# Linformer attention and a gated feed-forward net on one core: gates and every output block by seven products, attention outputs multiplied from PSUM, and an order of instructions and banks that a list scheduler gives

## The chip, the cores and the metric

The kernel runs on one core of a Trainium2 chip. The metric is device time in microseconds (us) of one execution. Five engines share the work: TensorE (PE) multiplies, ScalarE (ACT) and VectorE (DVE) work elementwise on SBUF and PSUM, GpSimd (POOL) broadcasts rows and issues the loads on its queue, SyncE (SP) issues transposes, small gathers and the stores.

## What is computed

Eight batch entries, eight heads, 1024 positions, head size 64; keys and values are first projected to 64 rows, and the attention's result goes through a gated net:

```python
k_proj = einsum('ks,bhsd->bhkd', E, k)
v_proj = einsum('ks,bhsd->bhkd', F, v)
attn = softmax(matmul(q, k_proj^T) / sqrt(64))
x = matmul(attn, v_proj)             # -> (8192 tokens, 512)
gate = sigmoid(x @ w_gate)           # w_gate, w_val: (512, 1536)
out = (gate * (x @ w_val)) @ w_out   # w_out: (1536, 512) -> (8192, 512) float32
```

Matmuls take bfloat16 and add up in float32. The sigmoid is had from tanh(x/2), so hidden values are (tanh + 1) times the value product, and the factor 0.5 is put on at the output.

## The kernel before

**Tiling.** The 8192 tokens are 16 blocks of 512, two for each batch entry. A block needs, for each of 12 chunks of 128 hidden columns, a gate product and a value product (each 4 matmuls of 128x512), and then the output product over 1536. Twelve chunks are handled as three quads of four: a quad holds chunks 2q, 2q+1, 2q+6 and 2q+7, so that it is a 2x2 problem in halves of the columns, halves of the depth and halves of the tokens.

**Seven products.** The value half of a quad is done by Winograd's form of Strassen's scheme: seven products of half-size operands, each four matmuls of 128x256, in place of eight (`v_pieces`, L1502, with `v_product`, L1421). The operands are sums of weights (`vt_sums`, L1372, once) and of tokens (`xs_sums`, L1411, for each block). Sums of products are in part had by further accumulation in the same PSUM bank: a bank collects P1, then P2's relatives on top; ACT takes a copy of it in between (`v_snap`, L1470) and DVE adds another bank to that copy (`v_add`, L1473, recorded at L1476). DVE then multiplies by the gates (`hidden`, L1449, recorded at L1457). The output of blocks 1 to 15 goes the same way (`first_products` L1282, `last_products` L1301, `add_snap` L1264, recorded at L1267); the last block has an order of its own with one more bank (`final_products`, L1318). The **gates** are direct: `g_step` (L1484) does one chunk with four 128x512 matmuls and one tanh. **Block 0** is direct throughout, its output too (`oproj`, L1146: 12 matmuls of 128x512 for each 128 tokens).

**Attention of one entry** (`attention`, L801) is made while the net works on the entry before. Keys and values are projected in one bank (`kv`, L754; 64x64 tiles of the array); kpd is transposed by a DMA of SP into kpD; q is transposed by four DMAs of SP into qT (`transpose_q`, L741). Scores are 64x64 matmuls, four abreast in the array, exponentials by ACT; denominators by 32-wide tiles, reciprocals by DVE, gathered into rows by SP's DMAs and spread over the partitions by POOL (`spread`, L921, recorded at L926). The outputs of attention are kept by ACT in SBUF as xu (`x_half`, L991) and multiplied there by DVE with the spread reciprocals into xT (`mul`, L954, recorded at L958). Heads go in four pairs r = 0..3; three pairs' scores stand in one event, the fourth pair's scores with the first two outputs in the next, the outputs of the last two pairs in a third (`scores3`, `mixed3`, `outputs3`). Entry 1 is made in the first stage, with its keys transposed and its reciprocals spread by PE (`k_alone`, `bc`).

**What sets the order.** A `Plan` (L28) records operations with what they read and write and makes the semaphores; each engine runs its own in the order of recording. That order is written out by hand: the first entry's slots in `todo`, later entries six quads with hooks (`on`, L1656 and on), so a g_step stands between each two steps of a value quad. PSUM's eight banks are two rings, FF for the net and AA for attention and output, with free lists. `mm` (L264) records every matmul, `act` (L268) every ACT operation, `load` (L282) every load on POOL's queue, so in the profile nearly all matmuls have the line L264, and groups are told apart by tiles. (pF and pA are the banks, wG and wV the weights, vT their sums, xT the tokens, xS their sums, hT the hidden values, hS their sums, wT the sums of w_out.)

**Loads.** At the start POOL queues entry 0's keys, queries and values in halves, then the weights in pieces. `second_loads` (L1584) queues q, k, v of entry 1, asks SP for q's transposes, and then w_out, which waits for two of those transposes; then the library of the broadcast. Later entries' k waits for the four transposes of the entry before, since both lie in one area with the spread reciprocals.

Of the kernel before, what the change touches and what calls it, by code (L numbers as in the profile page):

```python
# [27 lines left out]
class Plan:  # L28
# [9 lines left out]
    def add(self, eng, fn, r=(), w=(), x=(), dma=None):  # L38
# [5 lines left out]
        def dep(o, raw):  # L44
            if o is op:
                return
            if o.eng == eng and o.dma is None:
                if eng == "PE" or (eng != "POOL" and not raw):
                    return
            deps[id(o)] = o  # L50
# [67 lines left out]

def bass_linformer_attn__then__ffn_glu_sigmoid_kernel(
# [15 lines left out]
    NR = H // 2  # L135
    SCALE = 1.0 / (DH ** 0.5)

    with contextlib.ExitStack() as es:
# [4 lines left out]

        vT = sbuf("vT", [P, 3, 2, DFF // 2], BF16)
        wT = sbuf("wT", [P, 4, NF // 2, 256], BF16)
        early = [vT[:, :, :, :].rearrange("p a b c -> p (a b c)")]
        used = [0]

        def within(shape, dtype):
# [41 lines left out]
        )  # L191
        kpd = sbuf("kpd", [64, H, 2, DH], BF16)
        kpD = sbuf("kpD", [P, H, DH], BF16)
        vpD = sbuf("vpD", [P, H, DH], BF16)
# [3 lines left out]
        rrow = (  # L198
            eT[:, :, :].rearrange("p n c -> p (n c)").bitcast(FP32)
            .rearrange("p (i c) -> p i c", i=4)  # L200
        )
        xu = sbuf("xu", [P, 8, 512], FP32)
        xT = [sbuf(f"xT{i}", [P, NI, 2, 512], BF16) for i in range(2)]

        wG = sbuf("wG", [P, NI, DFF], BF16)
        wV = sbuf("wV", [P, NI, DFF], BF16)
        wO = sbuf("wO", [P, NF, DM], BF16)
        sigs = [sbuf(f"sig{i}", [P, 2, 512], FP32) for i in range(3)]
        sig = [sigs[i][:, 0, :] for i in range(3)]
        hT = [sbuf(f"hT{i}", [P, NF, 512], BF16) for i in range(2)]  # L210
        ost = sbuf("ost", [P, 4, DM], FP32)
        hS = sbuf("hS", [P, 2, NF // 2, 256], BF16)
        snap = [EF[:, 0:512], EF[:, 512:1024], sbuf("snap2", [P, 512], FP32)[:, :]]
        vsnap = [sbuf(f"vsnap{i}", [P, 512], FP32) for i in range(3)]
        xS = [sbuf(f"xS{i}", [P, 4, 2, 256], BF16) for i in range(2)]

# [4 lines left out]
        FB, AB = (0, 1, 2, 3), (4, 5, 6, 7)  # L221

        plan = Plan()
        add = plan.add
# [10 lines left out]
        A0, A1, A2, A3 = AB  # L235
        F0, F1, F2, F3 = FB
# [8 lines left out]
        ffn, att = Ring(FB), Ring(AB)  # L245

        class Free(list):
            def take(self):
                return self.pop(0)

            def two(self):
                return [self.pop(0), self.pop(0)]

        FF, AA = Free(), Free()

        def mm(b, o, lhsT, rhs, r, start=True, stop=True, tp=None, tr=False, read=False):
# [7 lines left out]
            return add("PE", lambda e: e.matmul(o, lhsT, rhs, **kw), r=r, x=[("bank", b)])  # L264

        def act(o, i, r, w, b=None, func=AF.Copy, scale=1.0):
            x = [] if b is None else [("bank", b)]
            return add("ACT", lambda e: e.activation(o, i, func, scale=scale), r=r, w=w, x=x)  # L268

        def dve(fn, r, w, b=None):  # L270
            x = [] if b is None else [("bank", b)]
            return add("DVE", fn, r=r, w=w, x=x)

        def pool(fn, r=(), w=()):
            return add("POOL", fn, r=r, w=w)


        wg_v = moe_w_gate.rearrange("(i p) f -> p i f", p=P)
        wv_v = moe_w_val.rearrange("(i p) f -> p i f", p=P)

        def load(o, i, w, sem, r=()):
            add("POOL", lambda e: e.dma_start(o, i), r=r, w=w, dma=sem)  # L282
# [4 lines left out]
        def load_k(b, after=()):  # L287
            n = 0
            load(
                KV[n][:, :, :],  # L290
                k[b].rearrange("h (p t) d -> p h (t d)", t=NT),
                [("KV", n, 0), ("KV", n, 1)],
                f"KV{n}",
                r=(turned() if b >= 2 else []) + list(after),
            )

        def load_v(b):
            n = 1
            load(
                KV[n][:, :, :],  # L300
                v[b].rearrange("h (p t) d -> p h (t d)", t=NT),
                [("KV", n, 0), ("KV", n, 1)],
                f"KV{n}",
            )
# [10 lines left out]
        def load_q(b):  # L315
            load(
                Qb[:, :, :],
                q[b].rearrange("h (p t) d -> p h (t d)", t=NT),
                [("Q", hf, R) for hf in range(2) for R in range(2)],
                "Q",  # L320
            )
# [10 lines left out]
        WCH = (0, 256, 512, 768, 1024, 1280, 1536)  # L332

        def load_w(j, ih=None):
            c = slice(WCH[j], WCH[j + 1])
            ii = slice(0, NI) if ih is None else slice(2 * ih, 2 * ih + 2)
            for n, t, src in (("wG", wG, wg_v), ("wV", wV, wv_v)):
                load(
                    t[:, ii, c],
                    src[:, ii, c],  # L340
                    [(n, j, x) for x in ((0, 1) if ih is None else (ih,))],
                    f"{n}{j}" if ih is None else f"{n}{j}h{ih}",
                )


        def start_loads():
            for src, rows, n in ((E, slice(0, 64), "E"), (F, slice(64, 128), "F")):
                add(
                    "SP",
                    lambda e, src=src, rows=rows: e.dma_start(EF[rows, :], src[:, :]),  # L350
# [139 lines left out]

        def busy(n):
            for _ in range(n):
                mm(FB[3], bank[FB[3]][:, 0:P], ident[:, :], ident[:, :], ["ident"])

        def pairs(R):
            return slice(0, NR) if R is None else slice(2 * R, 2 * R + 2)

        def both(R):  # L500
# [1327 lines left out]
```

## Time and profile before

| what | value |
|---|---|
| time, median of 3 runs (lowest to highest) | 532.36 us (531.95 to 533.25) |
| span of the profiled execution, slowest core | 529.3 us |
| its own time outside the span | not given; the median is 3.1 us over the span |
| PE busy, start to last end | 5.5 to 526.2 us in the span |
| ACT and DVE, busy share | 58% and 79% |
| matmuls of gates: pF<-xT,wG 128x512 | 707 recorded, 186.8 us busy |
| DVE addition to a copy, L1476, 128x512 | 689 ns each |
| ACT copy of a bank to vsnap, 128x512 | 598 ns each |
| ACT tanh of a bank, 128x512 | 601 ns each |
| DVE multiplication xT<-xu,KVs, L958 | 1023 ns each |
| POOL broadcast, L926 | 1035 ns each |
| bytes over the DMA queues | 56.18 MB, mean 106 GB/s |

How to read it: the span runs from the first to the last instruction that the profiler recorded. "Busy" counts the time in which an engine has an instruction under way; as PE's matmuls are pipelined and their ends modelled, its busy time says little of its pace, and the pace is read from one start to the next. A group in the profile is all instructions of one line, engine, operation and tile; behind it stand the busy time, the mean of one, and what ended the idle time before. The share of the chain that ended last says which engine the end hangs on. A DMA's "us to landing" runs from its issue to its last byte. The clock column is the share of full speed that was granted to PE; it reads 1.00 in every stretch named here.

### The profile page before, as it was taken

The page shows a single profiled execution, that of the slowest core. Times are in us where ns is not written, and L with a number is a line of the kernel's source. Part 1 is how long each engine was busy: PE and PEld are TensorE (multiplying, and loading weights), DVE is VectorE, ACT ScalarE, POOL GpSimd, SP SyncE. Part 2 cuts the span into 40 slices and gives each one's busy share as a digit, 9 for nine tenths or more (in the row PEclk, how much of TensorE's full clock was granted, in tenths as well). Part 3 has the DMA queues.
Part 4 walks back from the last instruction along what each step waited for, and adds up shares of the span by engine and source line. Part 5 has one row for each costly group of instructions (what it writes and reads, how often), then busy time and mean ns, then how long its engine had stood idle before and what let it go on. Part 6 is the DMA issues. An engine that isn't in the chain of part 4 may idle for free.

```text
span 529.3 us, 10415 instructions
## 1 busy us (share of the span) xinstructions
PE 515.5 (97%) x4110; PEld 350.8 (66%) x4173; DVE 416.3 (79%) x681; ACT 307.2 (58%) x551; POOL 133.4 (25%) x148
## 2 busy tenths in 40 slices
PE   5999999999999999999999999999999999999997
PEld 4545646656857667585766767576685867677676
DVE  4549786788987788877988779877888788997855
ACT  2565753688385564946468474764838564554541
POOL 9310200106700085001920048100650009200000
PEclk9999999999999999999999999999999999999999
DMA  9999999994393255911589223962620020202022
GB/s 167 199 199 202 155 213 195 184 171 89 35 230 60 82 91 84 231 53 38 90 157 162 80 40 57 213 105 80 88 86 1 0 83 3 80 1 79 1 81 80
DMA packets 77154, 56.18 MB, mean 106 GB/s; under 512 B 34801, under 2 KB 69297, under 8 KB 77105
## 3 DMA queue, kind: packets, MB, share of 16 engines
q0 software_dynamic: 33984, 29.89, 36.6%
q1 hardware_dynamic: 43120, 25.63, 19.4%
q8 instruction: 32, 0.52, 0.4%
q14 instruction: 18, 0.14, 0.1%
HBM read 60.29 MB, written 16.78 MB: 146 GB/s over the span
## 4 chain that ended last, share of the span: by engine, by line
PE 90%; DMA 7%; issue 1%; POOL 1%; DVE 0%; ACT 0%; POOLq 0%
PE pF L264 59%; PE pA L264 31%; DMA wO<-in_moe_w_out_dram 2%; DMA qT<-Qb 2%; DMA KVs<-in_v_dram 2%; POOL KVs L282 0%; POOL Qb L282 0%; DVE rden L639 0%; DVE vsnap L1476 0%; ACT vsnap L268 0%; DVE ost L1338 0%; POOL quad L356 0%; POOLq L102 0%; POOLq L1813 0%
## 5 line engine op out<-in xcount | busy, mean ns | idle before, releaser
L264 PE MATMUL pF<-xT,wG 128*128 128x512 bf16 x707 | 186.8, 379 | 3.8 <-DMA wG<-in_moe_w_gate_dram 0.2
L926 POOL PARTITION_BROADCAST KVs<-eT x96 | 96.8, 1035 | 243.5 <-PE pF L264 190.7
L268 ACT ACTIVATE sig<-pF 128x512 f32<-128x512 f32 x192 | 115.4, 601 | 49.3 <-PE pF L264 47.3
L1476 DVE TENSOR_TENSOR vsnap<-pF,vsnap 128x512 f32<-128x512 f32 x135 | 93.0, 689 | 39.7 <-PE pF L264 29.5
L264 PEld LDWEIGHTS pF<-xT,wG 128*128 128x128 bf16 x768 | 74.2, 98 | 54.5 <-issue 1.7
L268 ACT ACTIVATE vsnap<-pF 128x512 f32<-128x512 f32 x135 | 80.7, 598 | 46.9 <-PE pF L264 42.4
L1457 DVE SCALAR_TENSOR_TENSOR hT<-sig,vsnap 128x512 bf16<-128x512 f32 x135 | 93.5, 693 | 6.2
L264 PE MATMUL pF<-xT,wV 128*128 128x256 bf16 (+1 forms) x408 | 66.9, 286 | 0.0
L264 PE MATMUL pA<-wO,hT 128*128 128x256 bf16 x534 | 63.4, 273 | 0.0
L264 PEld LDWEIGHTS pA<-wO,hT 128*128 128x128 bf16 x534 | 52.1, 98 | 6.6 <-DVE ost L1267 0.3
L264 PE MATMUL pF<-xS,wV 128*128 128x256 bf16 x360 | 54.1, 273 | 0.3
L264 PEld LDWEIGHTS pF<-xT,wV 128*128 128x128 bf16 x408 | 38.2, 98 | 23.9 <-issue 5.7
L264 PE MATMUL pF<-xS,vT 128*128 128x256 bf16 x360 | 54.0, 273 | 0.0
L264 PEld LDWEIGHTS pF<-xS,wV 128*128 128x128 bf16 x360 | 34.3, 98 | 25.6 <-DVE vsnap L1476 5.0
L958 DVE TENSOR_TENSOR xT<-xu,KVs 128x512 bf16<-128x512 f32 x48 | 47.4, 1023 | 1.2 <-POOL KVs L926 0.7
L268 ACT ACTIVATE EF<-pA 128x512 f32<-128x512 f32 x30 | 17.9, 597 | 46.9 <-PE pA L264 46.9
L264 PE MATMUL pA<-wT,hT 128*128 128x256 bf16 x360 | 44.2, 273 | 0.0
L264 PE MATMUL pA<-wT,hS 128*128 128x256 bf16 x360 | 41.7, 273 | 0.0
L264 PEld LDWEIGHTS pA<-wT,hT 128*128 128x128 bf16 x360 | 35.1, 98 | 7.4 <-ACT snap L268 0.3
L264 PEld LDWEIGHTS pA<-wT,hS 128*128 128x128 bf16 x360 | 35.1, 98 | 4.3 <-issue 0.2
L264 PEld LDWEIGHTS pF<-xS,vT 128*128 128x128 bf16 x360 | 35.2, 98 | 4.1
L1267 DVE SCALAR_TENSOR_TENSOR ost<-pA,EF 128x512 f32<-128x512 f32 x29 | 20.0, 688 | 19.8 <-PE pA L264 19.7
(113 smaller groups left out, 487.6 us busy)
## 6 DMA issues: line engine op xcount, KB each, us to landing
out_dram<-ost SPq DMA_DIRECT2D x60, 256.0 KB, 2.4
Qb<-in_q_dram POOLq DMA_DIRECT2D x7, 1024.0 KB, 20.5
KVs<-in_k_dram POOLq DMA_DIRECT2D x7, 1024.0 KB, 12.0
KVs<-in_v_dram POOLq DMA_DIRECT2D x7, 1024.0 KB, 16.2
wO<-in_moe_w_out_dram POOLq DMA_DIRECT2D x1, 1536.0 KB, 12.3
wG<-in_moe_w_gate_dram POOLq DMA_DIRECT2D x5, 256.0 KB, 17.9
wV<-in_moe_w_val_dram POOLq DMA_DIRECT2D x5, 256.0 KB, 18.5
KVs<-in_k_dram POOLq DMA_DIRECT2D x2, 512.0 KB, 7.8
```

The source lines that it names most:

```text
L264: return add("PE", lambda e: e.matmul(o, lhsT, rhs, **kw), r=r, x=[("bank", b)])
L268: return add("ACT", lambda e: e.activation(o, i, func, scale=scale), r=r, w=w, x=x)
L926: lambda e, n=n, i=2 * rnd + c, j=j, parts=parts: e.partition_broadcast(rb[0:parts, n, :], rrow[32 * j : 32 * j + 1, i, :], channels=parts),
L958: lambda e: e.tensor_tensor(xT[s][:, r, :, 256 * g : 256 * g + 256], xu[:, n, :].rearrange("p (f c) -> p f c", f=2), y.rearrange("p (f c) ...
L1267: lambda e: e.scalar_tensor_tensor(o, bank[bk][:, :].rearrange("p (j c) -> p j c", j=2), 0.5, snap[n].rearrange("p (j c) -> p j c", j=2), ...
L1457: lambda e: e.scalar_tensor_tensor(o, sg[:, :, cc], 1.0, x.rearrange("p (j c) -> p j c", j=2), ALU.add, ALU.mult,),
L1476: lambda e: e.tensor_tensor(o, bank[bk][:, :], o, ALU.add),
```

## The change

The kernel computes the same; `kernel(...)` and the start up to the first tokens of block 0 are kept. What differs:

1. **Gates by seven products** for blocks 1 to 15, as the value half. One function, `seven`, does both. P1 is made in bank a; ACT copies it **from PSUM to PSUM** into a bank c, and PE adds the product A12·B21 onto the copy there, in place of a copy to SBUF and a DVE addition. A `clean` bank is one whose last use was a full one. The gates' weight sums are new (tW["G"]; 24 sums of weights in all instead of 8 wider ones).

```diff
-        def g_step(K, n):
-            for i in range(NI):
-                mm_one(blk, m, i, "G", bk)
-            act(sg[:, n % 2, :], bank[bk][:, :], ..., func=AF.Tanh, scale=0.5)
+        def seven(W, K, pos, step, done):
+            a, c, f = new_bank(), new_bank(clean=True), new_bank()
+            u2, u3 = new_buf(), new_buf()
+            pe(0, a, "A11", "B11", start=True)
+            job("ACT", pos, lambda: act(PB(c)[:, :], PB(a)[:, :], [], [], b=a, to=c))
+            pe(1, c, "A12", "B21")
+            done(0, 0, c, None, pos + step * 1)
+            pe(2, a, "S2", "T2")
+            snap(2, u2)
+            pe(3, f, "S1", "T1", start=True)
+            pe(4, a, "S3", "T3")
+            snap(4, u3)
+            job("DVE", pos + step * 4, lambda: plus(u3, f))
+            done(1, 1, None, u3, pos + step * 4)
+            pe(5, a, "A22", "T4", stop=True)
+            done(0, 1, a, None, pos + step * 5)
+            pe(6, f, "S4", "B22", stop=True)
+            job("DVE", pos + step * 6, lambda: plus(u2, f))
+            done(1, 0, None, u2, pos + step * 6)
+
+            seven("G", K, pos, STEP, gate)        # gate: one tanh for each quarter
+            seven("V", K, pos + LAG, STEP, value) # value: the multiplication into hT
```

2. **All sixteen output blocks by seven products** (`o_jobs`), block 0 and the last too, with the same copy from PSUM to PSUM; two of the quarters leave by ACT (`leave`), two by DVE (`merge`). `oproj` and `final_products` are gone.

```diff
+        def o_jobs(blk, pos, step, last=False):
+            pe(0, a, "A11", "B11", start=True)
+            job("ACT", pos, lambda: act(PB(c)[:, :], PB(a)[:, :], [], [], b=a, to=c))
+            pe(1, c, "A12", "B21")
+            s_jobs(4, pos + step * 1, ((0, 6),))
+            leave(1, c, 0, 0)
+            pe(2, a, "S2", "T2")
+            snap(2, u2)
+            pe(3, f, "S1", "T1", start=True)
+            pe(4, a, "A21", "T3")
+            snap(4, u3)
+            merge(4, u3, 1, 1)
+            pe(5, a, "A22", "T4", stop=True)
+            leave(5, a, 1, 0)
+            pe(6, f, "A12", "B22", stop=True)
+            merge(6, u2, 0, 1)
```

3. **Attention's outputs are multiplied from PSUM**: eight copies of ACT an entry go; DVE reads the bank. Scores and outputs are one event for each pair of heads (`score_jobs`, `out_jobs`), so eight events and the denominators' own in place of three. The gathered rows lie over the area of q (in place of that of the exponentials), and vpD is there twice. Entry 1 takes its own way, with reciprocals spread by PE (`out_jobs_pe`) and a key transpose by DMA as the other entries have it.

```diff
-                        xu[:, n, :].rearrange("p (f c) -> p f c", f=2),
-                        y.rearrange("p (f c) -> p f c", f=2),
+                        PB(bk)[:, :].rearrange("p (f c) -> p f c", f=2),
+                        yy.rearrange("p (f c) -> p f c", f=2),
```

4. **Order, banks and buffers by a list scheduler.** Each `job` has an engine, a position (in quads) and, for some, a release time; costs follow formulas, and banks (any of 8) and buffers (any of 13) are taken when a job starts. `run` goes through time and lets each engine that is free start the open job of the lowest position that is ready and has its banks, up to 1.3 positions ahead of PE. `safe` refuses a taking that could leave all waiting.

```diff
+        sched = Scheduler(range(8), range(2 + NB), 20.2, 1.3)
+    def run(self):
+        self.busy = {e: self.t0 for e in engines}
+        self.pipe = self.t0
+    def place(self, j, t):
+        j.end = t + j.cost + self.TAIL[j.eng]
+        if j.dma:
+            begin = max(self.pipe, t + j.cost + 1.3)
+            self.pipe = begin + j.bytes / 390e3
+            j.end = self.pipe + 0.9
+        # costs: PE (n / 2.4 + 2.4) / conc ns; ACT n / 1.2 + 60; DVE n / rate + 71
```

Weights have a table of landing times (`LAND`, 21.0 to 38.5) that releases block 0's and the weight sums' jobs.

5. **The loads of the stage after the start** stand in another order on POOL's queue, and none of entry 1's waits for transposes; entry 2's k waits for the four transposes of q of entry 1, as later ones do.

```diff
-        def second_loads():
-            load_q(1)
-            load_k(1)
-            load_v(1)
-            transpose_q()
-            load(wO[:, :, :], ..., r=turned()[:2])
+        job("POOL", 0.0, lambda: load_kv(0, k, 1))
+        job("POOL", 0.1, lambda: load_kv(1, v, 1))
+        job("POOL", 0.2, load_o)
+        job("POOL", 0.3, lambda: load_q(1))
+        job("POOL", 0.4, library)
+        kv_jobs(1, 3.4)
+        turn_q(3.5)
+        loads_kv(2, 3.6, turned())
+        score_jobs(1, 4.3, 0.1)
+        job("POOL", 4.5, lambda: load_q(2))
+        out_jobs_pe(1, 4.9, 0.1)
```

6. `Plan.add` records, for engines other than PE, also the waits of an operation on earlier ones of its own engine that it overwrites or whose input it overwrites.

## Prediction

> **What bounds the kernel now.** I read the page's busy line and chain first, then busy time in stretches, the PE timeline, and the DMA issues.
>
> ```profile
> PE 515.5 (97%) x4110; PEld 350.8 (66%) x4173; DVE 416.3 (79%) x681; ACT 307.2 (58%) x551; POOL 133.4 (25%) x148
> ```
> ```profile
> PE 90%; DMA 7%; issue 1%; POOL 1%; DVE 0%; ACT 0%; POOLq 0%
> ```
> PE is busy all the time and is 90% of the chain. The stretches from the first gate matmul, a stage of 87 us and then one steady period (two blocks of 512 tokens), are, in columns (length, then busy PE, PEld, DVE, ACT, POOL, granted clock, DMA share, GB/s):
>
> ```profile
> 20.51:107.46 86.95, 85.63 (x653) 48.27 (x664) 63.12 (x110) 49.46 (x91) 8.92 (x10) 1.00 1.21 192
> ...
> 232.88:295.54 62.66, 62.19 (x488) 43.19 (x496) 51.62 (x80) 38.50 (x70) 18.49 (x19) 1.00 0.53 104
> ```
> In the period PE is never short of work, and DVE has 11 us free. In the first stage the DMA queues run full (192 GB/s against 104). So time is PE's work, plus what PE waits for; the first stage is where loads could make it wait. Next the PE timeline (start, length to the modelled last end):
>
> ```profile
> 272.91 0.60 PE L264 MATMUL pF<-xS,wV 128*128 128x256 bf16 x4
> 273.44 0.41 PE L264 MATMUL pF<-qT,kpD 64*64 64x512 bf16 x4
> 273.68 0.60 PE L264 MATMUL pA<-qT,kpD 64*64 64x512 bf16 x8
> 274.22 0.61 PE L264 MATMUL pF<-xT,wV 128*128 128x256 bf16 x4
> ...
> 276.62 1.03 PE L264 MATMUL pF<-xT,wG 128*128 128x512 bf16 x4
> 277.48 0.60 PE L264 MATMUL pF<-xS,wV 128*128 128x256 bf16 x4
> 277.92 0.60 PE L264 MATMUL pF<-xS,vT 128*128 128x256 bf16 x4
> ```
> What counts is from start to start: four 512-wide matmuls take 0.86 (0.216 each), four 256-wide 0.44 (0.109 each; 24 between 290.96 and 293.58 give 0.109 too). And a change of the array's tiling costs: from 272.91, four 256-wide (0.43) end at 273.34, the twelve 64x64 matmuls go four abreast (3 x 0.216 = 0.65), yet the next start is 274.22. That is 0.23 over for two changes, 0.113 each. The piece from 240.92 to 244.41, with four changes, is 0.46 over, the same.
>
> **The products.** Seven products of four 256-wide matmuls for each quad (3 a block) replace 48 512-wide gate matmuls of a block: 48 x 0.216 = 10.38 becomes 84 x 0.109 = 9.16, 1.22 less. It holds for the gates of 15 blocks and the output of block 0: 16 x 1.22 = **-19.5**. Each is on PE, so on the path.
> The Trainium skill (TensorE: Matmul & The Clock Gate, Back-to-back issue gap) speaks against this: it gives 131 ns for a 512-wide matmul in a sustained stream and 81 for 128, so, as an estimate, 98 for 256, and a block would lose 84 x 0.098 - 48 x 0.131 = 1.9, some 31 us in all. The rows above show 216 and 109, and they decide.
>
> **Tiling changes.** Before, three score or output pairs stand together (three events a batch entry). After, each pair is an event of its own, placed where its banks came free. In the instruction orders of both kernels I count 92 changes of tile size on PE before and 173 after: 81 x 0.113 = **+9.2**. Bounds: 0, if the weight loads of the new tiling hid (in the rows they don't), and 12 with 0.15 each.
>
> **The other engines in the period.** DVE gains 12 gate additions (0.689 each) and loses two output merges and 8 x (1.02 - 0.68) on the multiplications that now read PSUM: 51.6 + 8.3 - 1.4 - 2.7 = 55.8 of 61.6 us. ACT gains three drains for a quad and one for a block and loses eight keeps: 38.5 + 18 x 0.6 + 1.2 - 4.8 = 45.7. Both fit, so **0**; but DVE has now only 6 us of air. Between a product and the matmuls that need its drain, the order of after leaves 1.09 us of PE work in most cases; the path in the trace (the product's start at 238.32, its last start-to-start end 238.75, ACT from 238.96 to 239.56, PE again at 239.62) takes 0.87. Added waits on a full semaphore list are hidden there. If the cover went, each 0.1 us on 15 x 6 + 16 copies would cost 10 us.
> The copies from PSUM to PSUM have no row; the nearest is ACT from PSUM to SBUF, 0.598 for 512. I take that; below, nothing to gain (they are covered); above, one end with 0.1 us too long, +10.
> The last block's tail (products, one merge 0.69, store 2.4) is the same to half a us: **0**.
>
> **The first stage, where the order of loads changes.** POOL's one queue lands loads in order:
>
> ```profile
> 31.50 0.89 POOL L282 DMA_DIRECT2D Qb<-in_q_dram  x1 [13.21 <-PE pF L264]
> 32.38 0.88 POOL L282 DMA_DIRECT2D KVs<-in_k_dram  x1
> 33.24 0.90 POOL L282 DMA_DIRECT2D KVs<-in_v_dram  x1
> ```
> with these times to landing (last column):
> ```profile
> Qb<-in_q_dram POOLq DMA_DIRECT2D x1, 1024.0 KB, 11.9
> KVs<-in_k_dram POOLq DMA_DIRECT2D x1, 1024.0 KB, 16.3
> KVs<-in_v_dram POOLq DMA_DIRECT2D x1, 1024.0 KB, 22.7
> ```
> The last weights (wV, issued 17.42, 21.0 to landing) are in at 38.4; q of entry 1 lands at 43.4, k at 48.7, v at 55.9: 5.2 us for each 1024 KB, 7.3 while q's transposes run beside it. After, the queue holds k1, v1, w_out, q1, v2, k2, and k2 is issued only when all four transposes of q1 have landed. The scheduler's transfer pipe starts empty at 20.2 us; the real one is full of weights until 38.4. So: v1 lands at 48.7, w_out (1536 KB) at 56.5, q1 at 61.7. The transposes of q took 12.6 us to the first landing beside loads (SP timeline from 43.42) and 4.4 alone (from 87.69); beside v2 I take 68 for the first and 72.5 for the fourth (with k's transpose between them). Then k2 is issued, and is in at 79.5 (5.2 for its bytes, 1.8 for issue and start; the k load issued at 96.38 took 12.0 beside stores, so up to 84.5).
> Against that stands where PE wants them. I count PE's work ahead by the pitches above; in the trace of before PE runs 10.0 us behind this count at 57.5 and 11.3 at 71.1 (the start), say 10.6. After: keys and values of entry 1 are wanted at work 34.3 (time 44 to 45) but come at 48.7; the scores of entry 1 at 46.2 (57) but their q at 68; entry 2's keys at 55.6 (66.2) but k2 at 79.5. Nothing else of PE's is in front, its order is fixed, so the three waits add to 79.5 - 66.2 = **+13.3**. Bounds: by bytes alone (38.4 + 5 x 5.2 + 7.8 = 72.2) 6.0; with k2 at 84.5, 18.3. In the trace of before, entry 2's keys are wanted only at 82.57.
> Then entry 1's outputs, in a row with no products between: after the key matmuls ACT does kpd (1.0), two vpD (1.2) and eight drains (8 x 0.5, start to start), DVE eight multiplications (0.62) and, among them, three weight sums (0.95) which the first output product waits for. From that order I get 9 us from the end of the key matmuls to the output product, with 2.7 us of PE work in it: 6.3 at most, 0 at least (DVE's pieces might be earlier, as PE's waits let it catch up). I take **+4.5**. DVE's 6 us of further weight and token sums of this stage lie in PE's waits: 0.
>
> **Sum.** The span is 529.3 and the median 532.36, so 3.1 lie outside the span (the profiled execution's own time isn't given). -19.5 + 9.2 + 13.3 + 4.5 = +7.5, less 0.4 for fewer small matmuls of entry 1's keys: 529.3 + 7.1 = 536.4, and **539.5** with the 3.1.
> The skill's same page (What's actually happening) says an idle window of about 3.4 us halves PE's clock. The trace shows only the start: 18 matmuls of 128 columns from 7.20 to 9.23 at 0.113 each, ten from 10.59 at 0.06, though the granted clock reads 1.00 over the stretch. By that rule the waits cost up to 1.7 us each more, 541 to 544. It is not in the sum.
>
> **Rivals.**
> *The loads are no bar* (ends on the other side). If k2 is in by bytes alone (72.2) and the outputs' row costs nothing, 532.4 - 10.7 + 6.0 = 527.7; if no wait at all is added, 521.7. It decides from k2 landing about 8 us earlier than I say and DVE's sums out of the way. For it: before's waits of PE in this stage are under 1 us. Against: the queue's landing times and the dependence of k2 on the transposes.
> *The tiling changes are free*: 9.2 less, 530.3. Against it stand three places in the trace.
> *DVE or the copies become the bound in the period*: DVE at 55.8 of 61.6, or copies 0.1 too long, gives 10 us more, 549. For it: 90% leaves little air; against: DVE ops of 0.69 start 0.60 apart.
> *The seven products don't save* (PE waits at each): at most what they save, 559; the output's seven products before run at full pitch, which speaks against it.
>
> **Chances.** Forecast (534 to 545) 0.58; loads no bar, wholly or mostly (521 to 531) 0.19; between, from free tiling or half the waits (531 to 534) 0.11; over 545 0.12. Slower by over 0.3% (1.6 us, about what a measurement here can tell from no change) 0.70, faster 0.19, the same 0.11. The range from 527 to 548 leaves out half of the loads' rival and of the slow end.
>
> **What would show it.** Right: PE idle before the KVs and qT matmuls with DMA as releaser, some 13 us between 44 and 80; a steady period near 61.1 + 0.5; PE's 256-wide pitch 0.109 throughout. Wrong: a stage without DMA waits; a period over 63 with DVE or ACT as releaser; ACT copies into PSUM well over 0.6.

## The result: slower by 3.4%, and the profile after

The changed kernel takes **550.53 us** (548.39 to 551.10, 4 runs) against 532.15 (531.84 to 533.25, 4 runs): a ratio of 1.0338, with a 95% interval from 1.0316 to 1.0359. The forecast was 539.5 and its range ended at 548, so the direction was right and the size was not. Two executions about two and four times as long as the others of their kernels (1055.71 us of the four with short broadcasts, 1903.34 us of the kernel before beside them) are left out of all comparisons. First the page of the changed kernel: span, busy times, and the shares of the chain that ended last.

```profile
span 548.8 us, 11581 instructions
...
PE 515.9 (94%) x4721; PEld 408.8 (74%) x4725; DVE 420.8 (77%) x728; ACT 360.0 (66%) x657; POOL 112.6 (21%) x148
...
PE 80%; DMA 10%; DVE 4%; ACT 3%; issue 1%; POOL 1%; SPq 0%; DVEq 0%; ACTq 0%; POOLq 0%
```

PE's busy time is that of before (515.5), but it now covers 94% of a longer span, and the chain has DMA, DVE and ACT in it. Busy time in stretches, columns as in the prediction (the 7th is the granted clock):

```profile
22.68:109.36 86.68, 72.48 (x566) 43.09 (x567) 60.53 (x116) 47.46 (x87) 6.53 (x8) 0.90 1.15 185
...
90.00:100.00 10.00, 8.09 (x56) 5.54 (x53) 8.85 (x15) 2.73 (x5) 0.53 (x1) 0.66 0.99 174
...
181.40:243.81 62.41, 61.44 (x569) 50.25 (x568) 50.55 (x85) 44.33 (x82) 15.03 (x19) 1.00 0.60 105
```

The first stage has 72.5 us of PE in 86.7, where before had 85.6 in 87.0, and a clock of 0.90 on the whole, 0.66 in its worst ten us. The period is 62.41 us here, 62.21 before it and 63.20 behind it; it was 62.66 before and should have been about 61.6. The PE timeline shows the first stage's two places. Around the first scores of entry 1:

```profile
68.41 0.64 PE L496 MATMUL pF<-qT,kpD 64*64 64x512 bf16 x4 [7.00 <-DMA kpD<-kpd]
68.98 1.04 PE L496 MATMUL pF<-xT,wG 128*128 128x256 bf16 x4
69.81 1.06 PE L496 MATMUL pA<-xS,tV 128*128 128x256 bf16 x4
...
73.04 0.60 PE L496 MATMUL pA<-xT,tV 128*128 128x256 bf16 x4
```

PE stands for 7.0 us, and then four matmuls take 0.83 to 0.86 from start to start instead of 0.44 (the granted clock is 0.50 from 66.0 to 72.8 us, and again from 86.5 to 96.7). From entry 2's keys to the first output product:

```profile
82.04 1.92 PE L496 MATMUL pA<-KVs,EFT 128*64 128x512 bf16 x16 [0.59 <-DVE rden L1550]
83.89 0.39 PE L496 MATMUL pF<-wT 32*128 32x256 bf16 x4
...
93.87 2.74 PE L496 MATMUL pF<-wO,hT 128*128 128x256 bf16 x12 [1.91 <-DVE wT L1299]
96.40 1.63 PE L496 MATMUL pF<-wT,hS 128*128 128x256 bf16 x12
```

Ten us from the end of the key matmuls to the first output product, which itself runs at half pace (2.53 from start to start where 1.31 is usual).

**One sum for all.** Count PE's work as in the prediction (pitches, 0.113 for each change of tile size) and see how far the trace runs behind that count ("behind" is the time of a matmul's start less all work counted ahead of it; the matmuls whose records the traces lack, 63 before and 4 after, are counted in). It gives, in us:

| | before | after | difference | predicted |
|---|---|---|---|---|
| work by the count | 509.1 | 498.4 | -10.7 | -10.7 |
| behind the count at 110 us (first stage) | 13.2 | 35.0 | +21.8 | +17.8 |
| added from there to 30 us before the last matmul (periods) | 3.0 | 8.5 | +5.5 | 0 |
| added in the last 30 us (tail) | 0.6 | 2.5 | +1.9 | 0 |
| from the last weight load to the span's end | 3.5 | 4.5 | +1.0 | 0 |
| span | 529.3 | 548.8 | +19.5 | +7.1 |

The experiments take this apart.

### The profile page after: what moved, and what is told of

Its sections match the earlier page's. It is cut to its first block, busy times and chain, and to the rows that moved or that the text cites. A ratio compares the mean times of both kernels' runs of the same rounds, so it can differ in the third digit from the quotient of the medians.

```text
span 548.8 us, 11581 instructions
## 1 busy us (share of the span) xinstructions
PE 515.9 (94%) x4721; PEld 408.8 (74%) x4725; DVE 420.8 (77%) x728; ACT 360.0 (66%) x657; POOL 112.6 (21%) x148
## 4 chain that ended last, share of the span: by engine, by line
PE 80%; DMA 10%; DVE 4%; ACT 3%; issue 1%; POOL 1%; SPq 0%; DVEq 0%; ACTq 0%; POOLq 0%
PE pA L496 40%; PE pF L496 40%; DMA Qb<-in_q_dram 5%; DMA KVs<-in_v_dram 2%; DMA out_dram<-ost 2%; DVE spare L1196 1%; ACT spare L509 1%; DMA kpD<-kpd 1%; DVE hT L1264 1%; DVE hS L1314 1%; ACT kpd L509 1%; ACT eT L509 1%; ACT vpD L509 0%; DVE rden L1550 0%; DVE wT L1299 0%
## 5 line engine op out<-in xcount | busy, mean ns | idle before, releaser
L1574 POOL PARTITION_BROADCAST KVs<-Qb x96 | 76.2, 924 | 153.4 <-PE pA L496 84.8
L509 ACT ACTIVATE spare<-pA 128x512 f32<-128x512 f32 x134 | 78.6, 595 | 19.2 <-PE pA L496 17.7
L509 ACT ACTIVATE spare<-pF 128x512 f32<-128x512 f32 x131 | 76.8, 596 | 18.9 <-PE pF L496 17.3
L1196 DVE TENSOR_TENSOR spare<-pF,spare 128x512 f32<-128x512 f32 x76 | 52.0, 684 | 34.7 <-ACT spare L509 25.6
L1196 DVE TENSOR_TENSOR spare<-pA,spare 128x512 f32<-128x512 f32 x86 | 58.8, 684 | 25.5 <-ACT spare L509 13.8
L509 ACT ACTIVATE spare<-spare 128x512 f32<-128x512 f32 x80 | 50.2, 627 | 23.2 <-DVE spare L1196 23.2
L1264 DVE SCALAR_TENSOR_TENSOR hT<-spare 128x512 bf16<-128x512 f32 x73 | 53.0, 725 | 0.7
L496 PE MATMUL pF<-wO,hT 128*128 128x256 bf16 x288 | 40.2, 279 | 1.9 <-DVE wT L1299 1.9
L496 PE MATMUL pA<-xT,wG 128*128 128x256 bf16 (+1 forms) x217 | 36.4, 288 | 0.6 <-ACT pA L509 0.4
L496 PE MATMUL pA<-xT,wV 128*128 128x256 bf16 (+1 forms) x196 | 31.6, 284 | 0.0
```

The lines of the kernel that those rows point to most:

```text
L1196: lambda e: e.tensor_tensor(BF(s), PB(b)[:, :], BF(s), ALU.add),
L1264: lambda e: e.scalar_tensor_tensor(o, y.rearrange("p (j c) -> p j c", j=2), 1.0, x.rearrange("p (j c) -> p j c", j=2), ALU.add, ALU.mult,),
L1574: lambda e: e.partition_broadcast(rb[0:parts, n, :], rrow[32 * j : 32 * j + 1, i, :], channels=parts),
```

## The experiments

Twelve runs of eleven kernels follow, each kernel an edit of the changed one (550.5 us); the kernel before took 532.1 to 532.3 beside them. The theory after the result was: the products and the tile changes are worth what was priced; what is lost are waits of PE, in the periods by DVE beside POOL's broadcasts, in the first stage because there is nothing to fill PE's waits with. Rivals are named in the expectations.

### The waits of the period: broadcasts cut short

```diff
-                    rb[0:parts, n, :], rrow[32 * j : 32 * j + 1, i, :], channels=parts
+                    rb[0:parts, n, 0:16], rrow[32 * j : 32 * j + 1, i, 0:16], channels=parts
```

> The changed kernel with POOL's 96 broadcasts cut from 512 to 16 columns each (most of each row of reciprocals is not spread, so that the attention of entries 2 to 7 is left unscaled in most columns); the order on every engine stays the same. Theory A: the wait of 0.8 to 1.2 us that PE has in each period before the last gate product comes from DVE operations with both inputs in SBUF, which take 1.14 instead of 0.68 us beside a broadcast. Then these waits go: six periods, 5 to 8 us less, 543 to 546. Rival B: DVE is simply too full in the period (12 added gate additions), broadcasts or not: the waits stay, 549.5 to 551.

Measured: **544.04** (three executions; ratio to before 1.0223, 1.0193 to 1.0254), 6.5 less. The same kernel once more, for its profile:

> The same kernel as the run with 16-column broadcasts, for a profile of an undisturbed execution (most of each row of reciprocals is not spread). Theory A: DVE operations with both inputs in SBUF take 0.68 to 0.75 us throughout, none above 1.0; the wait before the gate's last product (matmuls of xS with wG at 135, 198 and 260 us in the changed kernel) is under 0.5 us. Rival B: that wait stays at 0.7 to 1.2 us.

Measured: 543.73 (one execution). DVE in one stretch of the changed kernel, under a run of broadcasts (POOL's lines first, the second with the shortest, median and longest of three of them in ns; DVE's behind them, PE's wait last):

```profile
185.47 12.39 POOL L1574 PARTITION_BROADCAST KVs<-Qb  x16 [19.11 <-PE pA L496]
```
```profile
L1574 POOL PARTITION_BROADCAST KVs<-Qb x3: 797/1208/1280, 193.1 to 194.9; - x3
```
```profile
193.72 0.68 DVE L1314 TENSOR_TENSOR hS<-hT 128x1024 bf16<-128x1024 bf16 x1
194.32 1.15 DVE L1264 SCALAR_TENSOR_TENSOR hT<-spare 128x512 bf16<-128x512 f32 x1
195.39 1.15 DVE L1314 TENSOR_TENSOR hS<-hS,hT 128x1024 bf16<-128x1024 bf16 x1
196.46 0.68 DVE L1264 SCALAR_TENSOR_TENSOR hT<-spare,pF 128x512 bf16<-128x512 f32 x1
197.06 0.68 DVE L1196 TENSOR_TENSOR spare<-pA,spare 128x512 f32<-128x512 f32 x1
```
```profile
197.79 0.61 PE L496 MATMUL pA<-xS,wG 128*128 128x256 bf16 x4 [0.93 <-DVE spare L1196]
```

And the same operations with short broadcasts, DVE, PE and then the whole period:

```profile
192.90 0.68 DVE L1264 SCALAR_TENSOR_TENSOR hT<-spare 128x512 bf16<-128x512 f32 x1
193.50 0.68 DVE L1314 TENSOR_TENSOR hS<-hS,hT 128x1024 bf16<-128x1024 bf16 x1
```
```profile
195.83 0.61 PE L496 MATMUL pA<-xS,wG 128*128 128x256 bf16 x4
```
```profile
180.43:241.85 61.42, 61.37 (x569) 50.26 (x568) 49.49 (x86) 44.36 (x82) 5.99 (x19) 1.00 0.55 107
```

An operation with one input in PSUM takes 0.68 beside a broadcast; two with both in SBUF take 1.15. DVE's addition that frees bank f comes late by that, and the gate's last product (xS,wG) waits. Without the long broadcasts the wait is gone and the three periods from 119 to 303 us are 61.42 to 61.45 us (the forecast said 61.6). Theory A holds; DVE is not too full as such, since it does the same work here.

One thing the theory leaves out: two inputs in SBUF are not enough, the order of the starts decides. The operation at 193.72 has both inputs in SBUF too, but starts 0.06 us ahead of a broadcast; it takes 0.68, and the broadcast takes 1.28 instead of 0.80. In the trace of the changed kernel 30 such operations start while a broadcast runs. The 12 that start 0.59 us or more after its start take 0.68. Of the others, the six that meet a broadcast that was not itself held up (it takes 0.80) all end 1.20 us after that broadcast's start: a start at 0.07 took 1.13, one at 0.29 took 0.91, one at 0.46 took 0.74. So the operation waits until the broadcast is some 0.52 us old.

### Do the products pay: direct gates

```diff
-            seven("G", K, pos, STEP, gate)
+            for i, half_, tok in ((1, 0, 0), (4, 1, 1), (5, 0, 1), (6, 1, 0)):
+                gate_direct(i, half_, tok)   # 8 matmuls of 256 columns, tanh from PSUM
```

> The changed kernel with the gates of blocks 1 to 15 by direct products again (32 matmuls of 256 columns for a quad in place of 28; the sums of gate weights, the gate's copies and its 90 additions on DVE are gone), all else and the scheduler as they are. If the seven products gave PE what I priced (0.437 us a quad), 45 quads cost 19.7 us more; the waits on DVE in the period shrink and a few weight sums go, some 6 to 10 us back: 559 to 564. Rival C, the products save nothing because PE waits for their drains: 545 or less.

Measured: **563.26** (1.0582, 1.0554 to 1.0610), 12.7 more. Its period:

```profile
184.53:248.55 64.02, 64.02 (x593) 52.38 (x592) 43.61 (x74) 35.97 (x64) 15.02 (x19) 1.00 0.53 102
```

64.02 is 2.60 over the undisturbed period of 61.42, and six quads by 0.437 are 2.62. So the gates' products give PE exactly what was priced; with the direct gates DVE has 43.6 us of work, PE never waits (64.02 of 64.02), and that returns some of it. Rival C falls.

### Do tile changes cost: two pairs in one event

```diff
-            for r in range(NR):
-                bks = [new_bank(), new_bank()]
+            for r in range(0, NR, 2):        # scores and outputs of entries 2 to 7
+                bks = [new_bank() for _ in range(4)]
```

> The changed kernel with two pairs of heads in one event for scores (entries 2 to 7) and outputs of attention (entries 2 to 7), four banks taken at once; PE's order then has 120 changes of tile size in place of 173, with the same matmuls. Theory F, a change costs PE 0.113 us wherever it stands: 53 changes are 6.0 us; waits for four banks may give some back: 3 to 6 us less, 544.5 to 547.5. Rival G, changes are free (the weight loads hide): 550 or more.

Measured: **541.82** (1.0172, 1.0148 to 1.0197), 8.7 less, more than expected. The period:

```profile
243.03:303.85 60.82, 60.62 (x570) 50.48 (x570) 51.08 (x85) 44.65 (x82) 15.52 (x19) 1.00 0.60 108
```

By the count 6.0 us come from the 53 changes; the waits in the periods shrink as well (from 8.5 to 4.4 behind the count), while the first stage is some 3 us longer in the profiled execution. The changes are told from the waits by the period: it is 0.60 shorter than the one without waits (61.42), though the long broadcasts run here, so eight changes less are worth at least that; at 0.113 they make 0.90, with 0.3 of waits left (PE is idle for 0.20). Rival G falls; that waits would be added was wrong, they became fewer.

### The first stage: place, landing times, order of the loads

The constants out of the place of w_out's sums:

```diff
         bsel8 = within([P, 4, 2, 64], BF16)
-        kp = within([P, NR, DH], BF16)
+        # bsel8, rhi, rhl now in a tensor of their own; kp stays
...
-        NB = 11
+        NB = 10
...
-                w += ["bsel8", ("kp", 0), ("kp", 1)]
-                w += [(k, R) for k in ("rhi", "rhl") for R in range(2)]
+                w += [("kp", 0), ("kp", 1)]
```

> The changed kernel with one thing moved: the constants and reciprocals with which PE spreads entry 1's reciprocals get a place of their own (for one of the 13 buffers), so that the sums of w_out no longer lie over them and need not wait for entry 1's outputs. The scheduler is unchanged and still takes its transfers to start at 20.2 us. Theory D: block 0's output by seven cannot start before entry 1's outputs are through only because of that overlay, and so nothing is there to fill PE's waits before the scores and in the outputs' row. Then the output products move ahead of or between them: 5 to 9 us less, 541 to 546. Rival E: the waits are due to the late landing of q and k2 alone: 549 or more.

Measured: **540.40** (1.0152, 1.0127 to 1.0177), 10.1 less: more than expected, on Theory D's side. The wait of 7.0 us before the scores is still there, but output products now stand from 73.5 us on, between the scores and in the outputs' row.

The scheduler given a pipe that is busy with weights until 38 us:

```diff
-        self.pipe = self.t0
+        self.pipe = 38.0
```

> The changed kernel with the scheduler's transfer pipe from 38.0 us alone (the constants still under the sums of w_out). Theory D: with landing times that fit, it moves other work ahead of the scores, but block 0's output stays shut out: 3 to 6 us less, 544.5 to 547.5, less than half of what it gives with the constants in their own place (15.7). Rival J: the wrong landing times are the whole cause and the place of the constants does not matter: 534 to 538.

Measured: **547.14** (1.0291, 1.0267 to 1.0316), 3.4 less, with the first output product at 90.9 us (93.9 in the changed kernel). Both together:

> As the run with the constants in their own place, and the scheduler's transfer pipe starts at 38.0 us, about when the weights are in, instead of 20.2, so that its positions fit the real landings; the loads' order is not touched. Theory D with this: PE fills the wait of 7 us before the scores with block 0's output products and no idle is long enough for half clock: 13 to 18 us less than the changed kernel, 532 to 537. Rival E (late landings alone): as the changed kernel, 548 or more, since every load stays as late as it is.

Measured: **534.83** (1.0055, 1.0035 to 1.0074), 15.7 less. What PE does before the first scores then:

```profile
65.86 1.47 PE L497 MATMUL pF<-wO,hT 128*128 128x256 bf16 x12
...
69.57 1.47 PE L497 MATMUL pF<-wT,hS 128*128 128x256 bf16 x12
```

Block 0's output products (w_out's tiles) stand where PE had been idle, though the scores are later than in the changed kernel (72.5 against 68.4). The stretch from 20 to 110 us of the changed kernel, of this one, and of the last kernel below (the place alone stands between, with 668 matmuls):

```profile
20.00:110.00 90.00, 74.88 (x607) 44.98 (x608) 62.36 (x120) 50.18 (x92) 7.15 (x8) 0.91 1.15 186
```
```profile
20.00:110.00 90.00, 84.02 (x728) 52.33 (x727) 68.08 (x131) 61.11 (x112) 7.13 (x8) 1.00 1.17 179
```
```profile
20.00:110.00 90.00, 85.30 (x754) 55.00 (x751) 69.91 (x133) 61.64 (x114) 7.15 (x8) 1.00 1.18 182
```

Matmuls started rise from 607 to 754. The loads come no earlier: entry 2's keys land at 81.4 us in the changed kernel, at 80.7 with the place alone, 80.8 with the pipe alone, 81.9 with both and 82.0 in the last kernel. PE has something to do meanwhile.

The other way to the same end undoes one part of the change:

```diff
-        o_jobs(0, 4.8, OSTEP * 0.5)
+        for tt in (2, 3, 0, 1):
+            o_direct(tt, 4.5 + 0.1 * (tt ^ 2))   # 12 matmuls of 128x512 each, into one bank
```

> The changed kernel with block 0's output by direct products again (48 matmuls of 512 columns, which need no sums of w_out), queued at a position just behind the first scores; all else as it is. By PE's count it costs 1.2 us more. Theory D: these products can stand before the scores and in the outputs' row, as they wait only for w_out and hT: 3 to 7 us less than the changed kernel, 543.5 to 547.5. Rival E (landings alone set the end of the stage): 550 to 552.

Measured: **543.66** (1.0218, 1.0201 to 1.0235), 6.9 less, though PE's work is 1.7 us more. The product that was to save 1.2 us on block 0 thus costs about 7, as long as it has to wait for the place of its sums.

And the order of the loads, the step on which my forecast rested:

```diff
-        job("POOL", 0.2, load_o, name="loado")
-        job("POOL", 0.3, lambda: load_q(1), name="loadq")
+        job("POOL", 0.2, lambda: load_q(1), name="loadq")
+        job("POOL", 0.3, lambda: (load_o()), name="loado", release=32.5)
```

> The changed kernel with one thing in another order: q of entry 1 is loaded ahead of w_out (as in the kernel before) instead of behind it. Theory L, the step of my prediction, that the lateness of q and k2 by itself sets the end of the first stage: q lands some 7 us earlier, the scores and k2 4 to 7 us earlier: 543.5 to 546.5. Theory D, what is missing is work for PE to fill with: w_out now lands later beside the transposes and the outputs' row stays without products: 548 to 554.

Measured: **554.03** (1.0424, 1.0400 to 1.0448), 3.5 *more*. SP's queue and PE's wait for k2:

```profile
53.15 16.23 SPq L1440 DMA_TRANSPOSE qT<-Qb  x4
69.44 1.26 SPq L1484 DMA_TRANSPOSE kpD<-kpd  x1
```
```profile
81.53 3.21 PE L496 MATMUL pA<-KVs,EFT 128*64 128x512 bf16 x16 [4.46 <-DMA KVs<-in_k_dram]
```

q lands at 53.1 instead of 61.6, but its transposes, now beside the load of w_out, take 12.2 and 15.1 us (the first two; 6.2 and 4.9 in the changed kernel). The last lands at 71.5 against 71.7, so k2 is in at 81.5 against 81.4: the edit did not bring it forward. The transpose of the keys, behind q's four on SP, lands at 72.3, so the first scores start at 72.38 against 68.41; k2 is then waited for, and the row of outputs is as empty as in the changed kernel (first output product at 97.92). So this order of loads is no cure. Whether an earlier k2 would be one (Theory L) was not put to the test by it.

### The half pace

```diff
+            if sched.now is None and not filled:
+                filled.append(1)
+                for _ in range(26):
+                    mm(bks[0], PB(bks[0])[:, :], ident[:, :], wW["G"][:, 0, 0:512], ...)
```

> The changed kernel with 26 matmuls of no use (512 columns, 5.6 us at full pace) put on PE just before the first scores of entry 1, where it stood idle for 7.0 us; their bank is overwritten afterwards. Theory H, the half pace after the scores (four matmuls of 256 columns in 0.86 instead of 0.44 us from 69 to 72.4) comes from the idle time: the pace is full there, 2 us are won at 73 us; by the end 0.3 to 2.1 us less, 548.4 to 550.2, as the landing of k2 at 81.7 may take part of it back. Rival I, it comes from something else at that time (the loads, the kind of matmul): the half pace stays, 550.5.

Measured: **551.59** (1.0373, 1.0350 to 1.0396): 1.1 more, which the spread of the runs does not tell from no change. PE:

```profile
61.83 5.56 PE L496 MATMUL pF<-wG,ident 128*128 128x512 bf16 x25
68.79 0.41 PE L496 MATMUL pF<-qT,kpD 64*64 64x512 bf16 x4 [1.40 <-DMA kpD<-kpd]
69.13 0.61 PE L496 MATMUL pF<-xT,wG 128*128 128x256 bf16 x4
...
82.66 1.92 PE L496 MATMUL pA<-KVs,EFT 128*64 128x512 bf16 x8 [2.92 <-DMA KVs<-in_k_dram]
```

The pace is full (0.6 to the modelled end of four, 0.45 from start to start), so the half pace does come from the idle time: Theory H holds for the pace. But nothing is won: what PE gains it then waits for k2, which lands at 82.6 (81.4 in the changed kernel), and the later stretch at a granted clock of 0.50 grew, from 81.4 to 101.9 us instead of 86.5 to 96.7. In the changed kernel the key matmuls start at 82.04, 0.7 us after k2 is in, so the half pace at 69 to 72 us cost at most that; the one at 94 to 98 us, with no wait behind it, cost 1.4 (24 output matmuls in 4.00 instead of 2.62).

### Together

The constants in their own place, the pipe from 38.0, the outputs of attention (not the scores) two pairs at a time, as in the diffs above, and:

```diff
-        STEP, LAG = 0.14, 0.45
+        STEP, LAG = 0.14, 0.4
-        o_jobs(2 * B - 1, NQ + 0.05, OSTEP)
+        o_last(2 * B - 1, NQ + 0.05)         # A12·B22 in two halves, each with its own bank
```

> What the runs so far point to, together: constants in their own place, the transfer pipe from 38.0 us, two pairs of heads in one event for the outputs of attention, values 0.40 instead of 0.45 of a quad behind the gates (a calculation of the order with the measured costs shows the waits on DVE beside the broadcasts gone at this lag), and the last block's output in the order of the kernel before (the last product in two halves). From the run with place and pipe (534.8): 24 changes less, 2.7; the waits of 1.1 us in five or six periods, 5 to 6; the tail 1 to 2: 524 to 528, faster than the kernel before by 4 to 8 us. Rival: the lag moves the waits elsewhere in the period: 530 to 533.

Measured: **531.67** (0.9994, 0.9976 to 1.0013): not the 524 to 528 expected, though the waits of the period did go (no wait before the gate's last product over 0.4). By the count the loss lies ahead of 110 us: 24.4 behind against 21.1 in the run with place and pipe, with 1.0 of it by 40 us, a wait of 2.7 for the split of entry 1's reciprocals and 0.9 for k2, whose matmuls then run at half pace (3.54 us for 16 instead of 1.92):

```profile
84.28 0.39 PE L497 MATMUL pF<-own 32*128 32x256 bf16 x4 [2.70 <-DVE own L882]
...
86.67 3.54 PE L497 MATMUL pF<-KVs,EFT 128*64 128x512 bf16 x16 [0.87 <-DMA KVs<-in_k_dram]
```

(In the last block A12·B21 stands second, where the kernel before has it fourth.)

```diff
-            job("PE", 0.05, lambda: h_xo(1, [a, b]), name="xo1")
+            job("PE", 0.05, lambda: h_xo(1, [a, b]), release=22.0, name="xo1")
...
-        kv_jobs(2, 5.4)
+        kv_jobs(2, 6.0)
...
-        o_jobs(0, 4.8, OSTEP * 0.5)
+        o_jobs(0, 5.1, OSTEP * 0.4)
...
-            o_jobs(2 * p - 1, base + 0.35, OSTEP)
+            o_jobs(2 * p - 1, base + (0.35 if p > 1 else 0.0), OSTEP)
...
-            pe(b, "A12", "B21", start=True, stop=True)
-            pe(c, "S1", "T1", start=True, stop=True)
+            pe(c, "S1", "T1", start=True, stop=True, ms=(0, 4))
+            pe(b, "A12", "B21", start=True, stop=True, ms=(0, 4))
+            pe(c, "S1", "T1", start=True, stop=True, ms=(4, 6))
...
+            pe(b, "A12", "B21", start=True, stop=True, ms=(4, 6))
```

> As the run of all edits together (531.7), with five more shifts of positions: the keys of entry 2 later (6.0 for 5.4, so that a late k2 is not waited for), the first output products of block 1 0.35 of a quad earlier, those of block 0 0.3 later, the second half of block 0's first outputs of attention from 22.0 us (behind the first gate matmuls), and the last block's products that need the last sums split in two so that others fill the wait. Expected: k2's wait of 1.1, the tail's 1.0 to 1.5 and some of the start's 1.0 gone: 528 to 530, faster than the kernel before by 0.4 to 0.8%. Rival: the bound of the first stage is the chain of entry 1 itself, and the time moves by less than 1 us: 531 to 532.

Measured: **526.87** (525.90 to 529.14; ratio 0.9910, 0.9890 to 0.9930), 0.9% faster than the kernel before and faster than expected. What each of the five shifts gave is not shown. Its page:

```profile
span 524.1 us, 11639 instructions
...
PE 508.5 (97%) x4725; PEld 406.9 (78%) x4725; DVE 421.1 (80%) x731; ACT 359.9 (69%) x656; POOL 113.0 (22%) x148
```

It is 18.4 us behind the count at 110 us, where the changed kernel is 35.0 and the kernel before 13.2. k2 is no longer waited for, but the keys of entry 3 are (1.2 us at 112.5); the waits of the last block's sums are gone.

## Why the prediction was wrong, point by point

1. **The products, -19.5: right for the gates** (18.3 of it). The period with direct gates is longer by 2.60 us for six quads; 2.62 was priced. The rival that they don't save falls. The other 1.2, for the output of block 0, turned into a loss (point 4).
2. **Tile changes, +9.2: right in size,** by the period with two pairs an event (0.60 shorter with eight changes less; 0.90 were priced, and 0.3 of waits are left in it).
3. **"The other engines in the period ... Both fit, so 0": this step failed**, +5.5. I asked whether DVE's 55.8 us fit into 61.6, found they do, and took the drains as covered. (50.6 were measured. My sum was too high: I added 12 gate additions a period, but the copy from PSUM to PSUM takes one addition a quad from the value half as well. There are 135 such additions before and 180 after, six more a period.) The rival "DVE or the copies become the bound" was priced at 10 us by fullness, which was not the cause either. What counts is when DVE is slow: for operations with two SBUF inputs that start while one of POOL's broadcasts runs. The profile of before had it in part: the multiplication L958 reads xu and the spread row, both in SBUF, at a mean of 1023 ns, and I took that for the price of reading SBUF. The mean hides two kinds, as the line's own view in the trace of before shows (minimum, median, maximum in ns):

```profile
L958 DVE TENSOR_TENSOR xT<-xu,KVs x48: 677/1146/1151, 128.9 to 456.8; 128x512 bf16<-128x512 f32 x48
```

   35 of the 48 start while a broadcast runs and take 1147 on average, the other 13 (one of them starts near a broadcast's end) about 685. But lying beside a broadcast was not enough there either: 30 operations hT<-sig,vsnap, with both inputs in SBUF, overlap broadcasts in that trace, and 28 of them take 0.68 or 0.69; from 125 to 129 us it is three of the four broadcasts beside them that take longer, 1.10 to 1.34. The change made the multiplications fast, as they now read PSUM, and in its order operations hT<-spare and hS<-hS,hT start inside broadcasts, ahead of additions that free the banks PE needs. The Trainium skill (SBUF — State Buffer, Who interferes with whom) says it: a DVE instruction with two SBUF inputs contends with a GpSimd instruction that reads SBUF, and one with at most one SBUF input, outside the modes with two ports, does not. Here 1.15 against 0.68 us in one stretch agree with it. The copies from PSUM to PSUM, the cost I had put a bound on, take 0.583 to 0.587 us, less than the 0.598 assumed.
4. **The first stage, +13.3 and +4.5: direction right, 4.0 too small net, and the reason only half right.** Landings were well placed: the scores' operands came at 68.4 (68 forecast), q at 61.6 (61.7). Entry 2's keys were used at 82.0 (79.5 forecast): k2 took 8.8 us, not 7.0, from its issue. At 40 us PE was already 2.3 further behind the count than in before (14.0 against 11.7; profiles of the edited kernels, with the same start but for one, give 12.4 to 15.5), which I had not priced, and its waits from there to the keys made 11.9 instead of 13.3. The row of outputs cost 6.6 by the count instead of 4.5, just beyond my upper end of 6.3 (it took 10.0 us, where I had 9; with the 2.7 us of work that I took off it is 7.3). Half pace at the end of the row, which I had named and kept out of the sum, took 1.4. So one of these terms was smaller than forecast and three were larger; they add up to the table's 21.8 within half a us.

```profile
KVs<-in_k_dram POOLq DMA_DIRECT2D x1, 1024.0 KB, 8.8
```

   The reason that failed: "Nothing else of PE's is in front, its order is fixed". True of this order, but I held the late loads for the whole cause. With entry 2's keys as late (80.7 to 82.0 us), 10.1 us come back when the output products may move ahead of entry 1's outputs, and 15.7 when the scheduler also has the pipe busy until 38 us. Block 0's direct output, which is not shut out, gives 6.9. What shuts the seven products out is an overlay: the sums of w_out lie over the constants and reciprocals that spread entry 1's rows, so block 0's seven products must come behind entry 1's outputs; the direct output of before needed no sums.
5. **The tail, 0: wrong by 2.9.** The first product of sums waits 1.2 for DVE, the fourth 0.7 for ACT (neither wait is left in the last kernel, with another order), and the last product is whole where before had halves:

```profile
536.05 0.39 PE L496 MATMUL pA<-wT,hS 128*128 128x256 bf16 x2 [1.20 <-DVE hS L1314]
...
541.92 1.48 PE L496 MATMUL pA<-wT,hT 128*128 128x256 bf16 x12 [0.69 <-ACT spare L509]
```

   I had compared the tails by their last merge and not by the order of their products.

These make the 12.4 us by which the span was missed: 4.0, 5.5, 1.9 and 1.0. The median lies 1.7 over the span, not 3.1, so that the time was missed by 11.0.

What stays open: each experiment on the first stage also reorders other work, so the shares of place and landing times (10.1 and 3.4 alone, 15.7 together) are those of whole schedules. How much of the first stage's remaining 5 us is the chain of entry 1 itself was not tried apart, and no run brought k2 in earlier with all else unchanged. Why PE is further behind at 40 us is open as well.

## What to carry to other kernels

Ask of a rewrite that saves matmuls not only whether the other engines' totals fit, but whether each drain is in time in the one stretch where its engine is slow; a group's mean in the profile can be two kinds, so split it by what runs beside it and by which of the two started first. Where PE waits for loads, look first for work that could fill the wait and for what shuts it out (a shared place in memory, a landing time that a scheduler believes), before moving the loads. A piece that loses a long cover, like block 0's direct output, may cost several times what its cheaper form saves.

## What the runs showed of the hardware

- A DVE operation with both inputs in SBUF took up to 1.15 us when it started while a broadcast ran (15 of 30 in the changed kernel over 1.0), against 0.68 alone; started 0.59 us or more after the broadcast's start, or just ahead of one, it took 0.68, and the next broadcast took 1.28 instead of 0.80. With one input in PSUM it took 0.68 beside broadcasts and alone.
- After 7.0 us of idle PE ran at half pace for about 4 us (four 256-wide matmuls in 0.86; granted clock 0.50 until 72.8), after 1.4 us of idle at full pace. The granted clock was 0.50 again from 86.5 to 96.7 us, although no single idle time in the ten us ahead of it was above 1.8 us: in the last 3.4 us before it, PE was busy for 1.6. The Trainium skill (TensorE: Matmul & The Clock Gate, What's actually happening) speaks of an idle window of about 3.4 us; the first case agrees, the second shows that the window need not be idle throughout.
- A copy by ACT from one PSUM bank to another took 0.583 to 0.587 us for 512 columns, about as one to SBUF (0.595).
